# Attention and a gated MLP in one kernel: visits of the late units in one piece, and row sums of the first units over a 65th column

## The chip, the cores and the metric

One core of one Trainium2 chip runs the whole kernel. The time is device time in microseconds (us) of one execution; a version's time is the median of its runs. The engines are named as the profile names them: PE (TensorE matmuls), PEld (its weight loads), DVE (VectorE), ACT (ScalarE), POOL (GpSimd), SP (SyncE, which issues DMAs).

## What is computed

```python
for c in range(nc):                       # 24 chunks of 32 queries, seq 768
    q_c = q[:, :, c_start:c_end]
    k_ctx = k[:, :, l_start:r_end]        # 16 keys before, the chunk, 8 behind
    k_full = np.concatenate([mem_k, k_ctx], axis=2)   # and 8 memory keys: 64
    scores = scale * np.matmul(q_c, k_full.transpose(0, 1, 3, 2))
    a = np.exp(scores - np.max(scores, axis=-1, keepdims=True))
    a = a / (np.sum(a, axis=-1, keepdims=True) + 1e-09)
    out[:, :, c_start:c_end] = np.matmul(a, v_full)
x = out.transpose(0, 2, 1, 3).reshape(B * S, H * D)   # 3072 x 512
rms = np.sqrt(np.mean(x * x, axis=-1, keepdims=True) + 1e-6)
xn = x / rms * rms_g
g, val = xn @ w_gate, xn @ w_val                      # 512 -> 1536
result = (g * sigmoid(g) * val) @ w_out               # 1536 -> 512
```

There are 4 batches of 8 heads with head size 64.

## The kernel before, in words

**Attention.** The work is cut into 32 units: a batch, half of its sequence and a pair of heads. A unit's scores (tile `s`) are 128 rows by 6 chunks of 64 keys. DVE takes the row maxima (`mx`), subtracts them (`pe`), ACT takes the exponential in place, DVE sums the rows (`r`), adds 1e-9, takes the reciprocal and multiplies; PE transposes (`pT`), ACT copies the transposed tiles into SBUF (`pt`), and PE multiplies with v (`o`). The first eight units (`NE` = 8) supply the tokens of blocks 0 and 1 and are done at the start; their sums are taken for two units at a time (128x12). The other 24, the late units, go as 12 pairs in "visits" in between the products of the MLP.

**MLP.** The 3072 tokens are eight blocks of 384. The products are done in a reduced format (fp32r) with each operand split into a high and a low part, so each product is three matmuls: `xh`, `xl` are the parts of x, `wh`, `wl` those of a weight, `hh`, `hl` those of the hidden activations. `pg` is the product with w_gate, `pv` the one with w_val (12 matmuls each for a block and a column tile), `po` the one with w_out (9). Blocks 2 and later split their x and their weights by other code (tiles `kh`, `ks`, `os`, `sh`), and the last four blocks go as two "supers" of two blocks each, whose products are combined to save some (`mga`, `mva`, `mge`, `mve` and so on).

**Order.** Each engine runs its instructions in program order. Up to the end of block 1's first products the order is one written list of tokens, `ORDER`: a letter is a step and its number the unit or tile. U loads q and k, V loads v, Z a weight; S, M, a, E, d, n, P, C/m, O are scores, maximum, subtraction, exponential, row sums with reciprocal, multiplication, transposes, copies, product with v. J (two ACT passes), F, f, I, H, L open, clamp, sign, shift, round and subtract a piece of weight; an `a` behind f puts the sign on ACT, otherwise it is DVE's.

The blocks 0, 2 and 3 then run by gaps: gap 2n lies after the n-th `pg`, 2n+1 after `pv`, 2n+1.5 after the `po` that follows it. `VISITS` says for each gap which steps of the late pairs come there: `p` (transposes of the older pair with ACT's copies), `s` (scores of the next pair with their maximum, subtraction and exponential), `o` (product with v of the older pair in two tiles `oe` and `oo`, ACT's copies of both into the MLP's input `xT`, the squares of the copies on ACT, their addition on DVE, and row sums and reciprocals for the newer pair), `n` (the norm). The second half's tile `oo` lies in the PSUM bank with the tag that `stage_o2` is given; `pg` and `pv` use the tags "g" and "v".

In the supers the order of visits is in a table of its own. There `late_r` has ACT square the copies and DVE add the squares at once.

Of the kernel before, what the change touches and what calls it, by code (L numbers as in the profile page):

```python
# [8 lines left out]
F32 = mybir.dt.float32  # L9
# [5 lines left out]
ALU = mybir.AluOpType  # L15
# [3 lines left out]
B, H, S, D = 4, 8, 768, 64  # L19
# [3 lines left out]
KC = NM + LC + CH + RC  # L23
DM, FF = 512, 1536
P = 128
# [4 lines left out]
NJ = NC // 2  # L30
# [4 lines left out]
NE = NG * 2  # L35
# [4 lines left out]
YMAX = 0x1DFE / 0x1000 * 2.0 ** -96  # L40


VISITS = {0: {1: 's', 5: 'ps', 5.5: 'o', 7: 'ps', 7.5: 'o', 9: 'n', 10: 'n', 11: 'n'}, 2: {5: 'ps', 5.5: 'o', 17: 'ps', 17.5: 'o', 19: 'n', 20: 'nn'}, 3: {3: 'ps', 3.5: 'o', 7: 'ps', 7.5: 'o', 9: 'n', 9.5: 'n', 10: 'n', 11: 'ps', 11.5: 'o', 15: 'ps', 15.5: 'o', 17.5: 'n', 18: 'n', 19: 'n'}}
PAIRS = ((1, 2), (3, 4), (5, 6), (7, 8), (0, 9), (10, 11))
NR = 30

# [21 lines left out]


ORDER = """  # L70
U0 U1 U2 Z U3 S0 U4 M0 a0 Z S1 U5 E0 S2 M1 a1 Z V0 E1 M2 J d0 U7 S3 fa V1 F S4 n1 a2 V2 n0 E2 V3 M3 J I U6 P0 a3 H
M4 S5 E3 f m0a F C0a d1 Z J P1 V4 O0 M5 m1a a4 C1a S7 a5 E4 n2 E5 n3 Q0 P2 B0 I O1 C2a d2 Z m2a V5 B1 P3 V7 H V6 D0
C3a L O2 m3a n4 Q1 L P4 B2 A1g D1 p0 C4a M7 S6 Q2 n5 J A2g a7 O3 M6 m4a F q0 a6 Q3 P5 f E6 A3g O4 E7 D2 C5a d3 p2 Q4
G3 m5a B3 O5 I B4 y0 n6 Z H q1 D4 B5 p1 D3 J P6 n7 p3 D5 P7 C6a f Q5 q2 m6a L Y0 m7a F O6 C7a A5 z0 f O7 Q6 r0 B6 I
q3 Q7 B7 A6 p4 Z h0 p5 A7 D6 G7 D7 p6 y1 H j0 p7 F q5 k0a I J q4 L Z q6 l0 H q7 F J Y1 f o0 L z1 F r1 I h1 g2 J f Z
j1 I H k1a Z L v2 fa l1 F r2 H I h2 o1 J Z j2 L H F f g3 k2a L J v3 r3 l2 I h3 f Z H g4 J L F j3 o2 I f Z H v4 k3a F
J l3 r4 o3 I h4 F Z fa L g5 j4 k4a I v5 J l4 Z r5 o4 h5 f H H L g6 j5 J F v6 r6 L k5a l5 g7 I h6 J Z o5 r7 j6 H f g8
L k6a fa l6 F v7 F I h7 I o6 Z H J j7 Z L v8 r8 k7a H l7 g9 F h8 L J f o7 j8 I v9 k8a Z H l8 r9 F h9 g10 J j9 L f
v10 I o8 r10 Z H f J F g11 k9a F l9 h10 o9 j10 r11 I g12 L Z k10a fa l10 H I v11 Z h11 L Z H J L o10 Z J F j11 f v12
k11a r12 J l11 f F g13 I F H I J L o11 h12 H j12 J L v13 F r13 k12a f fa f I g14 l12 H I L Z H o12 Z F h13 j13 I L Z  # L80
v14 k13a H l13 J r14 o13 h14 f J L F fa I g15 j14 k14a H v15 r15 l14 L h15 J F o14 I j15 R0 fa F g16 H I k15a L H
l15 v16 r16 L h16 o15 j16
"""


# [1 line left out]
def tile_kernel(ctx: ExitStack, tc: tile.TileContext, q, k, v, w_gate, w_val, w_out, rms_g, out, out_t):  # L87
    nc = tc.nc
    const = ctx.enter_context(tc.tile_pool(name="const", bufs=1))
    p1 = ctx.enter_context(tc.tile_pool(name="p1", bufs=1))  # L90
    p2 = ctx.enter_context(tc.tile_pool(name="p2", bufs=2))
    p3 = ctx.enter_context(tc.tile_pool(name="p3", bufs=3))
# [12 lines left out]
    early = early_cm.__enter__()  # L105
# [34 lines left out]
    st = {}  # L140
    pts = [early.tile([P, NT, 4, 2, CH], F32, name=f"pt{i}") for i in range(2)]
    late, late_cm = {}, {}

    def late_buffers(i):

# [86 lines left out]
    def stage_mb(u):  # L232
        d = st[u]
        s3, mx = d["s3"], d["mx"]
        if u >= NE:
            pe = p1.tile([P, NJ, KC], F32, name=f"pe{u}", tag=f"pe{u % 2}")
        else:
            if ("pe", u // 2) not in st:
                st["pe", u // 2] = early.tile([P, 2, NJ, KC], F32, name=f"pe{u}", tag=f"pe{u // 2 % 2}")
            d["pair"] = st["pe", u // 2]  # L240
            pe = d["pair"][:, u % 2]
        nc.vector.tensor_tensor(out=pe, in0=s3, in1=mx.unsqueeze(2).broadcast_to([P, NJ, KC]), op=ALU.subtract)
        d["p"] = pe

# [8 lines left out]
    def stage_da(u):  # L253

        if u >= NE:
            pe = st[u]["p"].unsqueeze(1)
            rr = p2.tile([P, 1, NJ], F32, name=f"r{u}", tag="r")
            st[u]["r"] = rr[:, 0]
        else:
            pe = st[u]["pair"]  # L260
            rr = early.tile([P, 2, NJ], F32, name=f"r{u}", tag="r")
            for i in range(2):
                st[u - u % 2 + i]["r"] = rr[:, i]
        if units[u][1]:
            nc.vector.memset(pe[64:P, :, NJ - 1, LC + CH:LC + CH + RC], 0.0)
        else:
            nc.vector.memset(pe[0:64, :, 0, NM:NM + LC], 0.0)
        pe, r = pe.rearrange("p u j k -> p (u j) k"), rr.rearrange("p u j -> p (u j)")
        nc.vector.tensor_reduce(out=r, in_=pe, axis=AX.X, op=ALU.add)
        nc.vector.tensor_scalar(out=r, in0=r, scalar1=1e-9, scalar2=None, op0=ALU.add)  # L270
        nc.vector.reciprocal(out=r, in_=r)

    def stage_db(u):
        pe, r = st[u]["p"], st[u]["r"]
        nc.vector.tensor_tensor(out=pe, in0=pe, in1=r.unsqueeze(2).broadcast_to([P, NJ, KC]), op=ALU.mult)

    def stage_p(u, tag=None):
        d = st[u]
# [34 lines left out]
                        on_pe(nc.tensor.matmul(o2[cp][64 * hh:64 * hh + 64, o:o + CH], lhsT=st[u]["v"][r, j, hh],  # L313
                                               rhs=pt[r, j, hh ^ u % 2], start=True, stop=True))

    def late_r(pair, x):

        g = units[pair[0]][2]
        o2 = st["o2"]
        for u in pair:  # L320
            st.pop(u)
        xc = x[g // 2].rearrange("p g (j c q) -> p g j c q", c=2, q=CH)
        for cp in (1, 0):
            nc.scalar.copy(xc[:, :, :, cp], o2[cp][:, 0:HT].rearrange("p (g j q) -> p g j q", g=2, q=CH))  # L324
        for i in range(g, g + 2):
            s = obuf(f"sq{i}")[:, 0:HT]
            nc.scalar.activation(s, x[i // 2][:, i % 2], AF.Square)
            if i:
                nc.vector.tensor_tensor(out=s, in0=s, in1=late["ss"], op=ALU.add)
            late["ss"] = s  # L330

    def late_n(x, parts=1):

# [215 lines left out]
    make_identity(nc, ident)  # L549
    for t in pts:  # L550
        nc.vector.memset(t, 0.0)
    nc.gpsimd.tensor_scalar(out=rg, in0=rg, scalar1=DM ** 0.5, scalar2=None, op0=ALU.mult)
    nc.vector.memset(mhalf, -0.5)
    nc.vector.memset(onef, 1.0)
# [14 lines left out]
    def late_steps():  # L569


        pairs = [(u, u + 1) for u in range(NE, len(units), 2)]
        for n in range(len(pairs) + 1):
            old = pairs[n - 1] if n else ()
            cur = pairs[n] if n < len(pairs) else ()
            new = pairs[n + 1] if n + 1 < len(pairs) else ()
            own = bool(old) and old[0] >= 3 * 2 * NG
            if old and old[0] % NG == 0:
                if old[0] // NG in (5, 7):
                    late_x["x"] = [p1.tile([P, 2, HT], F32, name="x1", tag="wy"),  # L580
                                   late["tmp"][:, 0:2 * HT].rearrange("p (g t) -> p g t", g=2)]
                else:
                    t = p1.tile([P, NKT, HT], F32, name="xT", tag="x")
                    late_x["x"] = [t[:, 0:2], t[:, 2:4]]
                late_x[old[0] // NG] = late_x["x"]
            x = late_x.get("x")
            if old:
                with tc.high_priority():
                    for i, u in enumerate(old):
                        stage_p(u, None if i or own else "g")  # L590
                    for u in old:
                        stage_c(u)
                yield "p"
            if cur:
                with tc.high_priority():
                    stage_s2(cur)
                    for u in cur:
                        stage_m(u)
                    for u in cur:
                        stage_e(u)  # L600
            for u in new:
                load_qk(u)
            if old:
                if cur:
                    yield "s"
                with tc.high_priority():
                    stage_o2(old, None if own else "v")
                    late_r(old, x)
            norm = late_n(x, 1 if cur else 2) if n and n % 2 == 0 else ()
            behind = ExitStack()  # L610
            if norm:
                with tc.high_priority():
                    next(norm)
                behind.enter_context(tc.issue_after(last_of(nc.vector)))
            if own and norm and cur:
                for u in cur:
                    load_v(u)
                yield "o"
                next(norm)
                yield "n"  # L620
                with tc.high_priority():
                    for u in cur:
                        stage_d(u)
                yield "d"
            else:
                with tc.high_priority(), behind:
                    for u in cur:
                        stage_d(u)
                for u in cur if n else ():
                    load_v(u)  # L630
                yield "o" if old else "s"
            for _ in norm:
                yield "n"
# [670 lines left out]
```

## Time and profile before

| what | value |
|---|---|
| runs | 652.34, 652.45 and 655.0 us, median 652.45 us |
| profiled execution | 652.04 us, of which the profile's span is 650.2 us |
| busy share of the span | PE 98%, PEld 93%, DVE 75%, ACT 56%, POOL 2% |
| chain that ended last | PE 94%, DMA 2%, ACT 2%, DVE 1% |

The profile shows the profiled execution; 1.84 us of its time lie around the span. A matmul's record begins where its columns begin to stream, and consecutive records overlap, so what a matmul costs is read from one start to the next.

### The profile page before, as it was taken

The page shows a single profiled execution, that of the slowest core. Times are in us where ns is not written, and L with a number is a line of the kernel's source. Part 1 is how long each engine was busy: PE and PEld are TensorE (multiplying, and loading weights), DVE is VectorE, ACT ScalarE, POOL GpSimd, SP SyncE. Part 2 cuts the span into 40 slices and gives each one's busy share as a digit, 9 for nine tenths or more (in the row PEclk, how much of TensorE's full clock was granted, in tenths as well). Part 3 has the DMA queues.
Part 4 walks back from the last instruction along what each step waited for, and adds up shares of the span by engine and source line. Part 5 has one row for each costly group of instructions (what it writes and reads, how often), then busy time and mean ns, then how long its engine had stood idle before and what let it go on. Part 6 is the DMA issues. An engine that isn't in the chain of part 4 may idle for free.

```text
span 650.2 us, 15459 instructions
## 1 busy us (share of the span) xinstructions
PE 638.2 (98%) x6110; PEld 603.9 (93%) x6110; DVE 489.4 (75%) x999; ACT 366.2 (56%) x691; POOL 13.8 (2%) x19
## 2 busy tenths in 40 slices
PE   6999999999999999999999999999999999999997
PEld 4789999999899999999999999999999999999997
DVE  6999899768698888876888865567679854544864
ACT  4998877744545546465565454555566443333463
POOL 0200000000000000000000000000000000000000
PEclk7999999999999999999999999999999999999999
DMA  8737544269797887265459998887878988887711
GB/s 322 295 131 258 191 162 162 111 221 322 222 383 284 302 303 266 79 208 204 134 168 368 356 314 289 268 285 223 264 224 275 302 275 253 255 252 253 251 36 73
DMA packets 94006, 155.14 MB, mean 239 GB/s; under 512 B 8048, under 2 KB 47344, under 8 KB 93936
## 3 DMA queue, kind: packets, MB, share of 16 engines
q1 hardware_dynamic: 91920, 150.93, 69.2%
q10 hardware_dynamic: 2016, 3.25, 1.4%
q8 instruction: 48, 0.79, 0.5%
q14 instruction: 22, 0.18, 0.1%
HBM read 114.03 MB, written 40.11 MB: 237 GB/s over the span
## 4 chain that ended last, share of the span: by engine, by line
PE 94%; DMA 2%; ACT 2%; DVE 1%; issue 0%; SPq 0%
PE po L529 16%; PE pg L473 16%; PE pv L473 15%; PE mga L1001 8%; PE pa L1084 8%; PE mva L1001 8%; PE pe L1084 4%; PE mge L1001 4%; PE mve L1001 4%; PE oe L313 2%; PE s L219 2%; PE pc L1084 2%; PE mvc L1001 2%; PE mgc L1001 2%; PE pT L282 1%; DMA ws<-in_moe_w_val_dram 1%
## 5 line engine op out<-in xcount | busy, mean ns | idle before, releaser
L473 PE MATMUL pg<-xh,wh_g 128*128 128x384 f32 x192 | 65.9, 343 | 0.0
L473 PE MATMUL pv<-xh,wh_v 128*128 128x384 f32 x192 | 64.9, 338 | 0.5 <-ACT xT L324 0.5
L473 PE MATMUL pg<-xh,wl_g 128*128 128x384 f32 x192 | 64.6, 337 | 0.0
L473 PE MATMUL pg<-xl,wh_g 128*128 128x384 f32 x192 | 64.6, 336 | 0.0
L473 PE MATMUL pv<-xh,wl_v 128*128 128x384 f32 x192 | 64.3, 335 | 0.0
L473 PE MATMUL pv<-xl,wh_v 128*128 128x384 f32 x192 | 64.2, 334 | 0.0
L1001 PE MATMUL mga<-x,r 128*128 128x384 f32 x288 | 58.0, 335 | 0.0
L1001 PE MATMUL mva<-x,r 128*128 128x384 f32 x288 | 57.7, 334 | 0.0
L529 PE MATMUL po<-wh_o,hh 128*128 128x512 f32 x141 | 55.9, 396 | 0.0
L529 PE MATMUL po<-wl_o,hh 128*128 128x512 f32 x141 | 55.6, 394 | 0.0
L529 PE MATMUL po<-wh_o,hl 128*128 128x512 f32 x141 | 55.6, 394 | 0.0
L1052 ACT CAST hho<-h 128x384 fp32r<-128x384 f32 x72 | 37.0, 514 | 32.7 <-PE pa L1084 19.0
L1001 PEld LDWEIGHTS mva<-x,r 128*128 128x128 f32 x288 | 50.6, 188 | 0.0
L1001 PEld LDWEIGHTS mga<-x,r 128*128 128x128 f32 x288 | 50.5, 188 | 0.1
L1084 PE MATMUL pa<-hho,r 128*128 128x384 f32 x192 | 50.3, 335 | 0.0
L1053 DVE TENSOR_TENSOR hlo<-h,hho 128x384 fp32r<-128x384 f32 x72 | 39.3, 555 | 13.3 <-ACT hho L1052 12.4
L181 ACT CAST hh<-t 128x384 fp32r<-128x384 f32 x45 | 23.2, 516 | 44.1 <-PE po L529 20.3
L473 PEld LDWEIGHTS pg<-xh,wh_g 128*128 128x128 f32 x192 | 36.1, 188 | 1.8
L473 PEld LDWEIGHTS pv<-xh,wh_v 128*128 128x128 f32 x192 | 36.0, 188 | 1.7 <-ACT xT L324 0.9
L473 PEld LDWEIGHTS pg<-xl,wh_g 128*128 128x128 f32 x192 | 36.1, 188 | 1.4 <-DVE xl L676 0.2
L473 PEld LDWEIGHTS pv<-xl,wh_v 128*128 128x128 f32 x192 | 36.0, 188 | 0.3
L473 PEld LDWEIGHTS pg<-xh,wl_g 128*128 128x128 f32 x192 | 36.0, 188 | 0.0
(195 smaller groups left out, 1561.3 us busy)
## 6 DMA issues: line engine op xcount, KB each, us to landing
r<-kg SPq DMA_DIRECT2D x84, 256.0 KB, 3.8
r<-kv SPq DMA_DIRECT2D x84, 256.0 KB, 3.6
r<-ko SPq DMA_DIRECT2D x84, 256.0 KB, 3.2
kv<-in_v_dram SPq DMA_DIRECT2D x24, 384.0 KB, 4.4
kv<-in_k_dram SPq DMA_DIRECT2D x24, 312.0 KB, 4.4
q<-in_q_dram SPq DMA_DIRECT2D x20, 192.0 KB, 4.2
ws<-in_moe_w_gate_dram SPq DMA_DIRECT2D x6, 512.0 KB, 3.7
ws<-in_moe_w_val_dram SPq DMA_DIRECT2D x6, 512.0 KB, 4.6
```

The source lines that it names most:

```text
L181: return nc.scalar.copy(out, in_)
L219: on_pe(nc.tensor.matmul(d["s"][a:a + CH, o:o + KC], lhsT=d["q"][r, c * CH:c * CH + CH], rhs=d["k"][r, c // 2, 40 * cp:40 * cp + KC], star ...
L282: on_pe(nc.tensor.transpose(out=t[:, i * P:(i + 1) * P], in_=pe[:, i * P:(i + 1) * P], identity=ident))
L313: on_pe(nc.tensor.matmul(o2[cp][64 * hh:64 * hh + 64, o:o + CH], lhsT=st[u]["v"][r, j, hh], rhs=pt[r, j, hh ^ u % 2], start=True, stop=True))
L473: on_pe(nc.tensor.matmul(ps[:, 0:HT], lhsT=weight(a, n, f, kt), rhs=xs[c][:, kt], start=kt == first and i == 0, stop=kt == last and i == 2))
L529: on_pe(nc.tensor.matmul(po[i], lhsT=h[a][:, i * P:(i + 1) * P], rhs=weight(c, "o", f), start=f == first and n == 0, stop=f == end and n = ...
L1001: on_pe(nc.tensor.matmul(bank[w, b], lhsT=r[:, a, kt], rhs=x[:, c, kt], start=bool(first) and kt == 0 and i == 0, stop=kt == 1 and i == 2, ...
L1052: nc.scalar.copy(hh, x)
L1053: nc.vector.tensor_tensor(out=hl, in0=x, in1=hh.bitcast(F32), op=ALU.subtract)
L1084: on_pe(nc.tensor.matmul(bank[c][i], lhsT=w[u][:, x, i * P:(i + 1) * P], rhs=uhl[u][y], start=p == 0 and n == 0 and m in (1, 2, 5), stop=p ...
```

## The change

Four things are changed. In blocks 0, 2 and 3 the step `o` moves from behind the `po` of its gap to the end of the visit ahead of it, at eight places, and its second tile moves from the bank of tag "v" to that of tag "g". In the supers, the addition of the squares of every second pair is held until the next visit (`hold`). For the first eight units the tile `pe` gets a 65th column, set to 1e-9 once at the start, so that the row sum includes it, and the multiplication writes to another tile (`pn`) from which the transposes read. And `ORDER` is another sequence of the same 465 steps; of the changes in it only the first line is shown. In it the second weight load stands ahead of the loads of unit 4, units 0 and 1 change places, and two of the signs move from DVE to ACT (`f` 19 and `fa` 8 become 17 and 10).

```diff
-VISITS = {0: {1: 's', 5: 'ps', 5.5: 'o', 7: 'ps', 7.5: 'o', 9: 'n', 10: 'n', 11: 'n'}, 2: {5: 'ps', 5.5: 'o', 17: 'ps', 17.5: 'o', 19: 'n', 20: 'nn'}, 3: {3: 'ps', 3.5: 'o', 7: 'ps', 7.5: 'o', 9: 'n', 9.5: 'n', 10: 'n', 11: 'ps', 11.5: 'o', 15: 'ps', 15.5: 'o', 17.5: 'n', 18: 'n', 19: 'n'}}
+VISITS = {0: {1: 's', 5: 'pso', 7: 'pso', 9: 'n', 10: 'n', 11: 'n'}, 2: {5: 'pso', 17: 'pso', 19: 'n', 20: 'nn'}, 3: {3: 'pso', 7: 'pso', 9: 'n', 9.5: 'n', 10: 'n', 11: 'pso', 15: 'pso', 17.5: 'n', 18: 'n', 19: 'n'}}
...
-U0 U1 U2 Z U3 S0 U4 M0 a0 Z S1 U5 E0 S2 M1 a1 Z V0 E1 M2 J d0 U7 S3 fa V1 F S4 n1 a2 V2 n0 E2 V3 M3 J I U6 P0 a3 H
+U1 U0 U2 Z U3 S1 Z U4 M1 a1 S0 U5 E1 S2 M0 a0 Z V0 E0 M2 J d0 U6 S3 n0 J V1 a2 P0 M3 U7 E2 n1 S4 C0a a3 m0a f V2 E3
...
+    pn = [early.tile([P, NJ, KC], F32, name=f"pn{i}") for i in range(3)]
+    pairs_pe = [early.tile([P, 2, NJ, KC + 1], F32, name=f"pe{i}") for i in range(2)]
...
-            if ("pe", u // 2) not in st:
-                st["pe", u // 2] = early.tile([P, 2, NJ, KC], F32, name=f"pe{u}", tag=f"pe{u // 2 % 2}")
-            d["pair"] = st["pe", u // 2]
-            pe = d["pair"][:, u % 2]
+            d["pair"] = pairs_pe[u // 2 % 2]
+            pe = d["pair"][:, u % 2, :, 0:KC]
...
-        nc.vector.tensor_scalar(out=r, in0=r, scalar1=1e-9, scalar2=None, op0=ALU.add)
+        if u >= NE:
+            nc.vector.tensor_scalar(out=r, in0=r, scalar1=1e-9, scalar2=None, op0=ALU.add)
         nc.vector.reciprocal(out=r, in_=r)
...
-        nc.vector.tensor_tensor(out=pe, in0=pe, in1=r.unsqueeze(2).broadcast_to([P, NJ, KC]), op=ALU.mult)
+        if u < NE:
+            st[u]["p"] = pn[u % len(pn)]
+        nc.vector.tensor_tensor(out=st[u]["p"], in0=pe, in1=r.unsqueeze(2).broadcast_to([P, NJ, KC]), op=ALU.mult)
...
+    def late_add(s):
+        nc.vector.tensor_tensor(out=s, in0=s, in1=late["ss"], op=ALU.add)
+        late["ss"] = s
+
-    def late_r(pair, x):
+    def late_r(pair, x, hold=False):
...
-            if i:
-                nc.vector.tensor_tensor(out=s, in0=s, in1=late["ss"], op=ALU.add)
-            late["ss"] = s
+            if not i:
+                late["ss"] = s
+            elif hold:
+                late["held"] = s
+            else:
+                late_add(s)
...
+    for t in pairs_pe:
+        nc.vector.memset(t[:, :, :, KC:], 1e-9)
...
                 with tc.high_priority():
+                    if "held" in late:
+                        late_add(late.pop("held"))
                     for i, u in enumerate(old):
                         stage_p(u, None if i or own else "g")
...
-                    stage_o2(old, None if own else "v")
-                    late_r(old, x)
+                    stage_o2(old, None if own else "g")
+                    late_r(old, x, own and n % 2 == 1)
```

How instructions now stand is shown at three places. First PE in the first of the eight visits, in block 0. `pT` are the transposes, `s` the scores, `oe`/`oo` the product with v, `po` the product with w_out. Only the first and last rows of each group are shown. Before:

```order
L282 MATMUL pT_1965<-ident,pe_1851 128x128 x3
L219 MATMUL s_1971<-kv_1648,q_1646 32x64 x2
...
L529 MATMUL po_788<-wh_o_1122,hh 128x512
...
L529 MATMUL po_790<-wh_o_1122,hl 128x512
L313 MATMUL oe_2044<-pt_1647,kv_1648 64x32 x2
...
L313 MATMUL oo_2045<-kv_1648,kv_1708 64x32 x2
L473 MATMUL pg<-xh_144,wh_g_1124 128x384
```

And of the change:

```order
L285 MATMUL pT_1964<-ident,pe_1850 128x128 x3
L221 MATMUL s_1970<-kv_1646,q_1644 32x64 x2
...
L316 MATMUL oe_2034<-pt_1645,kv_1646 64x32 x2
...
L316 MATMUL oo_2035<-kv_1646,kv_1707 64x32 x2
L539 MATMUL po_776<-wh_o_1133,hh 128x512
...
L539 MATMUL po_778<-wh_o_1133,hl 128x512
L483 MATMUL pg<-xh_151,wh_g_1135 128x384
```

The 24 small `oe` and `oo` rows have changed places with the nine `po`.

Next DVE near its start, at the row sums of the first pair of units and what follows them; `mx` are the maxima of later units, `wy` a piece of weight. Before:

```order
L230 TENSOR_REDUCE mx_266<-s_233 128x6
L267 MEMSET pe_199 64x2x16
L269 TENSOR_REDUCE r_271<-pe_199 128x12
L270 TENSOR_SCALAR r_271<-r_271 128x12
L271 RECIPROCAL r_271<-r_271 128x12
L422 TENSOR_SCALAR wy_268<-wy_268 128x512
L275 TENSOR_TENSOR pe_199<-pe_199,r_271 128x384
L242 TENSOR_TENSOR pe_335<-s_233,mx_266 128x384
L275 TENSOR_TENSOR pe_199<-pe_199,r_271 128x384
```

And of the change:

```order
L232 TENSOR_REDUCE mx_272<-s_239 128x6
L267 MEMSET pe_128 64x2x16
L269 TENSOR_REDUCE r_277<-pe_128 128x12
L272 RECIPROCAL r_277<-r_277 128x12
L278 TENSOR_TENSOR pn_125<-pe_128,r_277 128x384
L242 TENSOR_TENSOR pe_129<-s_239,mx_272 128x6x64
L232 TENSOR_REDUCE mx_321<-s_285 128x6
L278 TENSOR_TENSOR pn_126<-pe_128,r_277 128x384
```

The row L270 is gone, the clamp of a weight piece (L422) stands further back, and the products are written to `pn`.

Last DVE in the first super, at the first addition of squares there; `e` and `spare` are sums of PE's products. Before:

```order
L977 TENSOR_TENSOR e_5198<-mge,e_5198 128x384
L977 TENSOR_TENSOR spare<-mge,spare 128x384
L329 TENSOR_TENSOR sq_5298<-sq_5298,sq_5296 128x384
L977 TENSOR_TENSOR e_5219<-mve,e_5219 128x384
L984 TENSOR_TENSOR h_5125<-spare,e_5219 128x384
```

And of the change:

```order
L991 TENSOR_TENSOR e_5197<-mge,e_5197 128x384
L991 TENSOR_TENSOR spare<-mge,spare 128x384
L991 TENSOR_TENSOR e_5218<-mve,e_5218 128x384
L320 TENSOR_TENSOR sq_5297<-sq_5297,sq_5295 128x384
L998 TENSOR_TENSOR h_5124<-spare,e_5218 128x384
```

The sum `e` of `mve` now stands ahead of the addition of squares.

## Rows read from the trace of the kernel before

**Rows 1.** The page: busy time by engine; shares of the chain that ended last.

```profile
PE 638.2 (98%) x6110; PEld 603.9 (93%) x6110; DVE 489.4 (75%) x999; ACT 366.2 (56%) x691; POOL 13.8 (2%) x19
...
PE 94%; DMA 2%; ACT 2%; DVE 1%; issue 0%; SPq 0%
```

**Rows 2.** Windows, early stretch: length, busy PE, PEld, DVE, ACT, POOL; PEclk, DMA share, GB/s.

```profile
8.40:14.40 6.00, 4.32 (x144) 3.78 (x144) 5.01 (x12) 3.91 (x6) 0.00 (x0) 0.52 1.04 407
...
18.00:24.05 6.05, 5.05 (x127) 4.15 (x126) 5.89 (x14) 5.92 (x14) 0.00 (x0) 0.93 1.04 414
24.05:43.27 19.22, 19.12 (x252) 16.84 (x253) 18.62 (x40) 18.55 (x38) 5.66 (x5) 1.00 0.39 144
```

**Rows 3.** Waits of PE over the span: total, times, longest.

```profile
PE s L203 <- DMA k<-in_k_dram: 4.1, 5, 1.2
...
PE mve L1001 <- DVE e L977: 0.7, 1, 0.7
...
PE pv L473 <- ACT xT L324: 0.5, 1, 0.5
```

**Rows 4.** Timeline of DVE, 8 to 25 us: start, duration.

```profile
10.47 0.95 DVE L269 TENSOR_REDUCE r<-pe 128x12 f32<-128x768 f32 x1
11.45 0.17 DVE L270 TENSOR_SCALAR r<-r 128x12 f32<-128x12 f32 x1
11.66 0.23 DVE L271 RECIPROCAL r<-r 128x12 f32<-128x12 f32 x1
```

**Rows 5.** The chain that ended last, 8 to 46 us: start, duration.

```profile
6.73 7.22 DMA ws<-in_moe_w_val_dram
13.97 0.69 ACT ws L417
...
25.12 0.97 PE s L203 x48
```

**Rows 6.** The chain that ended last, 155 to 176 us: start, duration.

```profile
155.53 2.08 PE pv L473 x12
...
159.37 2.26 PE po L529 x9
...
163.17 2.32 PE pg L473 x12
165.49 0.47 ACT xT L324
...
166.01 2.35 PE pv L473 x12
```

**Rows 7.** Timeline of ACT, 208 to 217 us.

```profile
213.24 0.53 ACT L247 ACTIVATE pe<-pe 128x384 f32<-128x384 f32 x1 [0.76 <-DVE pe L242]
213.79 0.51 ACT L181 CAST hh<-t 128x384 fp32r<-128x384 f32 x1
214.21 0.52 ACT L247 ACTIVATE pe<-pe 128x384 f32<-128x384 f32 x1
...
215.92 0.49 ACT L324 COPY xT<-oo 128x384 f32<-128x384 f32 x1
```

**Rows 8.** Timeline of PE, 215.2 to 215.8 us.

```profile
215.44 0.45 PE L473 MATMUL pg<-xh,wh_g 128*128 128x384 f32 x1
```

**Rows 9.** Timeline of DVE, 319 to 328 us.

```profile
320.29 2.20 DVE L361 SCALAR_TENSOR_TENSOR xT<-xT,rg,rr 128x384 f32<-128x384 f32 x4
322.41 0.69 DVE L866 TENSOR_TENSOR os<-wh_o,wl_o 128x512 f32<-128x512 f32 x1
323.01 1.02 DVE L230 TENSOR_REDUCE mx<-s 128x6 f32<-128x384 f32 x2
```

**Rows 10.** Timeline of PE, 321.2 to 325.4 us.

```profile
321.40 0.50 PE L529 MATMUL po<-wh_o,hh 128*128 128x512 f32 x1
```

**Rows 11.** Timeline of DVE, 398 to 403 us.

```profile
400.64 0.56 DVE L329 TENSOR_TENSOR sq<-sq,sq 128x384 f32<-128x384 f32 x1 [2.83 <-ACT sq L327]
401.12 0.55 DVE L977 TENSOR_TENSOR e<-mve,e 128x384 f32<-128x384 f32 x1
```

More of the change, by code (lines that the diff above doesn't have):

```diff
@@ L70 @@
 ORDER = """
-U0 U1 U2 Z U3 S0 U4 M0 a0 Z S1 U5 E0 S2 M1 a1 Z V0 E1 M2 J d0 U7 S3 fa V1 F S4 n1 a2 V2 n0 E2 V3 M3 J I U6 P0 a3 H
[L72 to L80, printed above, removed]
@@ L81 @@
-v14 k13a H l13 J r14 o13 h14 f J L F fa I g15 j14 k14a H v15 r15 l14 L h15 J F o14 I j15 R0 fa F g16 H I k15a L H
-l15 v16 r16 L h16 o15 j16
+U1 U0 U2 Z U3 S1 Z U4 M1 a1 S0 U5 E1 S2 M0 a0 Z V0 E0 M2 J d0 U6 S3 n0 J V1 a2 P0 M3 U7 E2 n1 S4 C0a a3 m0a f V2 E3
+F fa P1 d1 S5 C1a M4 m1a I J O0 n2 Z a4 V3 P2 H M5 V5 S6 E4 F V4 n3 B0 a5 m2a L E5 C2a I O1 Q0 d2 H P3 V7 B1 V6 S7
+C3a D0 Z Q1 n4 O2 m3a D1 A1g J M6 P4 L Q2 O3 M7 m4a a6 A2g C4a p1 a7 Q3 n5 q1 E7 A3 P5 E6 B3 G3 d3 m5a O4 C5a B2 O5
+n6 B4 y0 F Q4 P6 D2 B5 q0 D4 m6a p2 D5 C6a p0 D3 Q5 Y0 n7 J F P7 A5 p3 z0 f C7a O6 I m7a O7 r0 Z B6 Q6 q3 Q7 A6 h0
@@ new lines @@
+q2 A7 p5 f G7 D6 p4 B7 j0 p6 H y1 D7 q5 k0a F q4 I q7 L Z H p7 f Y1 l0 q6 L z1 o0 J I r1 Z H F f h1 g2 J j1 L I fa F
+Z v2 r2 k1a J l1 I g3 H Z fa L F H I o1 h2 L Z J j2 r3 v3 k2a H l2 J f F o2 I L Z h3 f J g4 F j3 I k3a v4 H r4 Z H
+l3 L g5 f J L o3 h4 F fa j4 r5 F v5 I k4a Z l4 g6 I h5 H j5 Z J o4 r6 L f v6 k5a J l5 F I g7 h6 H Z j6 o5 r7 L v7
+k6a H l6 h7 L J o6 j7 f g8 fa F I v8 r8 Z H F I k7a J g9 l7 Z L h8 o7 H j8 F f v9 k8a r9 J l8 L o8 h9 F J j9 I g10 f
+Z k9a H v10 l9 fa r10 I L g11 Z F J I o9 h10 H r11 Z j10 L g12 k10a fa l10 F h11 I v11 H Z Z H L J o10 j11 J L F Z
@@ L83 @@
+r12 J v12 f f k11a f l11 g13 I h12 j12 H F J F v13 L I I H fa o11 L r13 F I g14 Z k12a J Z l12 h13 o12 H j13 fa F H
+I v14 k13a r14 Z l13 L h14 o13 L J j14 J f F g15 H f k14a l14 L v15 F J I r15 H F o14 I fa L R0 h15 I H g16 j15 H L
+k15a l15 v16 r16 L h16 o15 j16
 """
```

## The prediction

> **What bounds the kernel now.** The page first: PE is busy for 98% of the span and makes up 94% of the chain that ended last; DVE is at 75%, ACT at 56% [rows 1]. So PE's own work sets the time, and a change can gain only where PE stands idle, or where its matmuls run at a worse pace than the same matmuls elsewhere. The windows show where it stands. From 24.05 us on it is dense (19.12 of 19.22 us busy, and as dense behind). Ahead of that it is not: 4.32 of 6 us at a granted clock of 0.52 (the lower of TensorE's two levels, 1.2 GHz) in the stretch from 8.4 us, and 5.05 of 6.05 at 0.93 in the stretch up to 24.05, where DVE (5.89) and ACT (5.92) are both full [rows 2]. The waits of PE then name what is left: 4.1 us for the first loads of k, 0.7 us in a super for a sum `e` of DVE, 0.5 us for a copy `xT` of ACT [rows 3]. The last two are the only waits of note behind 24 us, and both stand beside steps that this change moves.
>
> The chain of the early stretch tells what sets the 24 us: the landing of the first piece of w_val (issued at 6.73 us, 7.22 us long), ACT's opening of it at 13.97, then ACT and DVE by turns until PE's dense work, in which the eighth unit's scores are 0.97 us at 25.12 [rows 5]. Loads run at full share of the DMA engines there (1.04, 407 GB/s) [rows 2].
>
> **The visits.** PE does transposes, scores, `po`, `oe`/`oo`, `pg`. Its own work stays the same. What differs is how often it goes from the small matmuls to large ones. Twelve `pv` in plain sequence take 2.08 us; the twelve `pg` behind `oe`/`oo`, which have the same size, take 2.32 [rows 6]. The break costs 0.24 us. `po` behind the scores (2.26 us for nine) pays a break of its own. After the change the small ones stand together, and only `po` behind them pays. I take the whole 0.24 eight times: -1.9 us. What bounds it: nothing, if `oe`/`oo` behind the scores pay for themselves (a change of operands between small ones is shown by no row), and 0.24 if they don't; I take the upper end since the small matmuls already change their operands at each row within the visit.
>
> The one wait on `xT` comes in this place too: `pg` ends at 165.49, ACT's copy `xT` ends at 165.96, and `pv` then takes 2.35 [rows 6], since it writes the bank of tag "v" from which that copy reads. With the second tile in the bank of "g" and a whole `po` behind it, `pv` need not wait for it: -0.5 of waiting, and a part of the 0.27 by which this `pv` is longer than the plain one. I take -0.6.
>
> The new wait is `pg`'s, since it now writes the bank that the copy of `oo` reads. In the visit at 210 us ACT does its exponentials at 213.24 and 214.21 with a cast `hh` between, and the copy of `oo` ends at 216.41 [rows 7]; `pg` starts at 215.44 [rows 8] and doesn't care, as it isn't its bank. In the changed order the cast is behind the copies. The exponentials start as before (they wait for DVE's subtraction of scores that are no earlier), 0.5 us each, so the second ends near 214.3, and two copies by 0.4 us start to start end near 215.05. `pT`, scores, `oe`/`oo` and `po` sum to the same, so `pg` would start at 215.4: it has about 0.36 us to spare. The Trainium skill, "PSUM — Partial Sum Buffer", section "PSUM bank collisions raise a hardware error", says that different engines may not touch one bank and group of partitions at once and that a semaphore has to guard it by bank, which is why even a copy that reads other columns would hold `pg`; by it alone the wait exists in all eight visits, and what it costs is the row's matter.
>
> One visit has nothing to spare. At 320 us DVE is held until 323.01 by four steps of the norm (2.20 us) and a sum for a weight (0.69) [rows 9]; the scores end by 321.4, when `po` starts [rows 10]. The maxima could start there and start 1.5 us later; the subtractions, exponentials and copies behind them are late by as much, and less the 0.36 to spare `pg` waits about 1.1 us. Behind `pg` on PE stands everything else, so this counts in full.
>
> **The held addition.** In the first super DVE has the addition of squares at 400.64, after 2.83 us of waiting for ACT's squares, and the sum `e` at 401.12 is queued behind it [rows 11]; PE's `mve` waits 0.7 us for `e` [rows 3]. The change puts `e` ahead of the addition, which itself waits for nothing at the next visit. So -0.7 us. Nobody needs the sum of squares before the norm of the second pair. The other supers have the same move without a wait to remove: 0.
>
> **The first units.** Removed are four additions of 1e-9 on DVE. One takes 0.17 us and holds its queue from 11.45 to 11.66, so 0.21 us [rows 4]; three lie ahead of the dense stretch: -0.63 us of DVE's queue. Two signs move from DVE to ACT, one addition from POOL to DVE; they lie behind 24 us, where PE is dense, and I cost them at nothing as long as the halves of the weights come before PE asks for them (if not, each is about half a microsecond). Two memsets of 128x12 at the start lie in DVE's wait for the first scores: nothing. The sums over 65 columns of 12 rows read 12 elements more out of 768; at 0.95 us for the 768 [rows 4] that is 0.015 us each: nothing.
>
> The order itself: the load of w_val goes ahead of unit 4's, by 512 KB at 407 GB/s 1.3 us earlier. But both openings now stand on ACT ahead of the second pair's exponentials and wait for that landing, near 12.7 us; by walking ACT's and DVE's queues with the rows' durations, the third exponential ends near 15.9 us, DVE idles about a microsecond there, and the multiplication before the fifth transpose comes at 23.9 us where it was 23.4. Against that the eighth unit's scores (0.97 us [rows 5]) have moved ahead of it into time in which PE stands idle, and one triple of `pg`/`pv` more (0.52 us) is done before the first `po`. I come to -0.45 us, and as bounds -2 (w_val's 1.3 us and the 0.63 both come through) and +1 (the microsecond on DVE is lost in full and the gains aren't).
>
> **Sum.** -1.9 -0.6 +1.1 -0.7 -0.45 = -2.55 us. From the profiled execution's 652.04 us (its span 650.2 and 1.84 around it) that is 649.5; the median of the runs shown is 652.45, 0.41 above it, and gives 649.9. I say 649.7. A measurement of this kernel can tell about 0.5% (3.3 us) from no change, so the forecast lies inside that.
>
> **Rivals.**
> *The early stretch gains the most of it.* The chain begins at w_val's landing [rows 5]; if that piece of chain just moves by 1.3 us and DVE loses its 0.63, dense work begins 1.5 us earlier than worked out above: 648.2 us. For it speaks that both DVE and ACT are full from 18 us on [rows 2], so each row taken off counts; against it, that the opening now stands in front of an exponential.
> *The visits give nothing.* The break is paid by `oe`/`oo` behind the scores, whose transposed operands come from ACT's copy only just before. Then 1.9 is lost: 651.6 us, and up to 652.5 if the early stretch loses its microsecond as well.
> *Rows of 65.* DVE's subtraction, sum and multiplication for the first units work on rows that begin at every other alignment. If these rows are slower, four steps of about 0.5 us and one of 0.95 for each pair lengthen; a pace lower by one eighth on 2.9 us costs 0.36 for a pair, 1.1 us for the three ahead of the dense stretch, against 0.63 saved: 650.8 us. No row here has such rows, and the bound below is nothing. The Trainium skill, "Vector Engine (DVE) Microarchitecture Reference", section "5.2 Measured stream behaviour on trn2 (trn3 not measured)", says that a port has its full pace only for pairs of neighbouring words that begin on an even word, and gives 1.30 ns a column for pairs on odd ones against 1.054. An estimate by that page, for half of the rows, is an eighth. No run here shows it yet.
> *Slower: `pg` waits for the bank at every visit.* If something is queued on DVE or ACT ahead of the copies in each, as in the visit at 320 us, `pg` waits 1.1 us at the other seven too: +7.7, 657.4 us. It decides (over 655.7) from 0.9 us a visit on. Against it stand the 0.36 us to spare by [rows 7, 8].
>
> **How the numbers follow.** The forecast (649.0 to 650.6) gets 0.47, the early gain 0.21, the visits without gain 0.16, rows of 65 0.10, the bank 0.06. Faster by over 0.5% (below 649.2): a fifth of the forecast (0.09) and nearly all of the early gain (0.20), 0.29. Slower by over 0.5%: the bank, and 0.01 for other things, 0.07. The rest is 0.64. The range reaches from a little below the early gain (647.6, with its bound of -2) to the end of the second rival (652.3).
>
> **What would show it.** `pg` behind a visit takes 2.1 us, `po` 2.26; no wait of `pv` on `xT` near 165; a wait of `pg` on ACT's `xT` of about 1 us near 325 and none above 0.2 elsewhere; no wait of `mve` on `e`; the first dense transposes near 24.4 us and the first `po` near 43.3. A `pg` that waits in most visits, or a start of the dense stretch off by over a microsecond, makes the prediction wrong.

## The result and the profile after

The changed kernel takes 657.22 us (median of 20 runs, 654.55 to 662.52), the kernel before 653.30 (20 runs, 652.26 to 655.07). The ratio of the two is 1.0058, 95% interval 1.0042 to 1.0074: slower, outside the predicted range, and on the side that had 0.07. The runs of the change also spread more than twice as far.

The profiled execution took 658.87 us, 1.65 above the median; its span is 656.8 us, 6.6 more than before's. Where they come from is read from one landmark of PE's timeline to the next; both executions are put side by side here (start in us of the first `po`, of the transposes of each of the eight visits, and of those of the first super):

```
             before   after   later by
first po      43.27   44.23     0.96
visit 1      157.46  158.33     0.87
visit 2      168.20  168.26     0.06
visit 3      209.80  210.53     0.73
visit 4      251.07  251.88     0.81
visit 5      286.82  290.08     3.26
visit 6      303.02  308.82     5.80
visit 7      319.56  325.16     5.60
visit 8      335.80  342.80     7.00
first super  376.34  383.84     7.50
end          650.20  656.80     6.60
```

Three visits lose nearly all of it: the fourth (at 251 us) 2.45, the fifth (290) 2.54, the seventh (325) 1.40. The second loses 0.67, against 0.81 that the first gains. The waits of PE name three releasers for them (total, times, longest):

```profile
PE s L205 <- DVE r L269: 1.7, 1, 1.7
PE oe L316 <- ACT kv L183: 1.4, 1, 1.4
PE pg L483 <- ACT x L331: 1.4, 1, 1.4
PE pT L285 <- issue: 1.2, 1, 1.2
PE oe L316 <- issue: 1.0, 1, 1.0
...
PE oo L316 <- issue: 0.6, 1, 0.6
```

Before, `pv`'s wait for `xT` and `mve`'s for `e` stood in this list [rows 3]; both are gone, as forecast. New are a wait of `oe` for ACT's copy `kv`, the forecast wait of `pg` for the copy of the second tile, and four waits for "issue": time in which PE waited for nothing that the profile shows. The early stretch, by windows (length, busy PE, PEld, DVE, ACT and POOL, granted clock, DMA share, GB/s):

```profile
8.40:14.40 6.00, 3.69 (x99) 2.91 (x94) 5.32 (x11) 2.72 (x5) 0.00 (x0) 1.00 1.04 400
...
18.00:24.05 6.05, 4.96 (x164) 3.94 (x157) 5.92 (x14) 5.90 (x13) 0.00 (x0) 1.00 1.01 381
24.05:43.27 19.22, 17.78 (x244) 16.38 (x233) 18.09 (x38) 17.48 (x36) 3.85 (x4) 1.00 0.35 124
```

The stretch behind 24.05 us, where PE was dense before (19.12 of 19.22 us, [rows 2]), now has 1.4 us of idle PE in it; 1.2 of them are one wait for "issue" within the three transposes of a unit.

The visit at 290 us on PE's timeline (start, duration, in brackets the idle time before):

```profile
292.37 0.23 PE L316 MATMUL oo<-kv,kv 64*64 64x32 f32 x2
293.57 0.25 PE L316 MATMUL oe<-pt,kv 64*64 64x32 f32 x2 [0.98 <-issue]
...
295.06 0.63 PE L539 MATMUL po<-wl_o,hh 128*128 128x512 f32 x1
295.49 0.63 PE L539 MATMUL po<-wh_o,hl 128*128 128x512 f32 x1
...
298.39 0.34 PE L483 MATMUL pg<-xh,wh_g 128*128 128x384 f32 x1
```

The product with v stops for about a microsecond in the midst of its small matmuls with both operands there. Behind it the nine `po` come 0.43 us apart, where they are 0.23 apart elsewhere: 3.75 us instead of 2.2. The windows of the `po` behind the visits at 251 and 290 us show why (PEclk is the granted clock):

```profile
core 0: us, PE busy (x) PEld busy (x) DVE busy (x) ACT busy (x) POOL busy (x), PEclk, DMA share, GB/s
256.76:260.34 3.58, 3.58 (x15) 2.79 (x10) 1.12 (x2) 2.69 (x7) 0.00 (x0) 0.58 1.00 316
294.64:298.39 3.75, 3.75 (x15) 2.94 (x10) 2.58 (x10) 1.90 (x5) 0.00 (x0) 0.54 1.00 325
```

The clock that was granted is near the lower of its two levels (1.2 GHz), after PE had stood idle for 1.4 and 1.0 us amid small matmuls. The visit at 251 us has its idle time from ACT, whose copy `kv` is queued behind a cast `kh` that waits for DVE:

```profile
252.84 0.47 ACT L183 COPY pt<-pT 128x384 f32<-128x384 f32 x1
254.39 0.40 ACT L860 CAST kh<-ks 128x256 fp32r<-128x256 f32 x1 [1.08 <-DVE ks L855]
254.71 0.47 ACT L183 COPY kv<-pT 128x384 f32<-128x384 f32 x1
```

```profile
255.23 0.25 PE L316 MATMUL oe<-pt,kv 64*64 64x32 f32 x2 [1.43 <-ACT kv L183]
```

At 325 us `pg` starts when ACT's copy of `oo` has ended (ACT, then PE), as the prediction worked out for this visit:

```profile
330.48 0.99 ACT L247 ACTIVATE pe<-pe 128x384 f32<-128x384 f32 x2 [2.63 <-DVE pe L242]
...
331.73 0.48 ACT L331 COPY x<-oo 128x384 f32<-128x384 f32 x1
```

```profile
332.26 0.44 PE L483 MATMUL pg<-xh,wh_g 128*128 128x384 f32 x1 [1.38 <-ACT x L331]
```

### The profile page after: what moved, and what is told of

The parts are those of the page before. It is cut to its first block, busy times and chain, and to the rows that moved or that the text cites. A ratio compares the mean times of both kernels' runs of the same rounds, so it can differ in the third digit from the quotient of the medians.

```text
span 656.8 us, 15458 instructions
## 1 busy us (share of the span) xinstructions
PE 640.4 (98%) x6110; PEld 607.9 (93%) x6110; DVE 488.1 (74%) x996; ACT 368.7 (56%) x693; POOL 12.3 (2%) x18
## 4 chain that ended last, share of the span: by engine, by line
PE 85%; DVE 7%; DMA 4%; ACT 2%; issue 1%; SPq 1%; DVEq 0%; ACTq 0%
PE pg L483 13%; PE po L539 13%; PE pv L483 12%; PE mga L1015 8%; PE pa L1098 8%; PE mva L1015 8%; PE mge L1015 4%; PE mve L1015 4%; PE pe L1098 4%; PE pc L1098 2%; PE mvc L1015 2%; PE mgc L1015 2%; PE oe L316 2%; PE s L221 2%; DMA kv<-qp 2%
## 5 line engine op out<-in xcount | busy, mean ns | idle before, releaser
L539 PE MATMUL po<-wh_o,hl 128*128 128x512 f32 x141 | 57.1, 405 | 0.0
```

What stands on the lines that cost most here:

```text
L539: on_pe(nc.tensor.matmul(po[i], lhsT=h[a][:, i * P:(i + 1) * P], rhs=weight(c, "o", f), start=f == first and n == 0, stop=f == end and n = ...
```

## Experiments

Two theories were put against each other at first, A: the visits lose the time by waits on other engines and on the bank; B: the early stretch does. A third, C, was that PE's waits for "issue" are the cause. All times are medians; the kernel before ran beside each (653.3 to 653.8 us).

**The visits alone** (`visits_only`), the early part and the held addition as before (all eight visits; only the first two are shown, here and in the next edit):

```diff
-... 5: 'ps', 5.5: 'o', 7: 'ps', 7.5: 'o' ...
+... 5: 'pso', 7: 'pso' ...
...
-stage_o2(old, None if own else "v")
+stage_o2(old, None if own else "g")
```

> The kernel before with only the visits changed (the eight products with v behind the scores, second tile in the bank of tag g). Theory A, the visits lose the time: o waits for ACT's kv copy behind a cast kh in the visits at 251 and 290 us, PE's clock falls to its lower level after such a wait, and pg waits 1.4 us for xT in the visit at 325 us; then 4 to 6 us slower than before. Theory B, the early stretch (new order and 65 columns) loses it: then 2 us faster than before. Theory C, idle times of PE that the profile calls issue come wherever small matmuls crowd: slower by 1 to 3 us, with such idle times in several visits.

657.77 us, ratio 1.0067 (1.0051 to 1.0083). **The early part alone** (`early_only`), which is the rest of the change without the held addition:

```diff
-... 5: 'pso', 7: 'pso' ...
+... 5: 'ps', 5.5: 'o', 7: 'ps', 7.5: 'o' ...
...
-stage_o2(old, None if own else "g")
+stage_o2(old, None if own else "v")
-late_r(old, x, own and n % 2 == 1)
+late_r(old, x)
```

> The change without its visits and without the held addition: the new order of the first blocks and the 65th column alone. Theory A: about 0.9 us slower than before, as the first po of the changed kernel came 0.96 us later. Theory B: 4 us slower. Theory C: up to 1.5 us slower, through the idle times of 1.2 and 0.3 us near 20 and 27 us.

652.96 us, ratio 0.9993 (0.9979 to 1.0006). B falls: the visits cost 4.2 us, and the early part alone differs from before by no more than its interval.

**Three visits put back** (`split3`):

```diff
-... 17: 'pso' ... 3: {3: 'pso' ... 11: 'pso' ...
+... 17: 'ps', 17.5: 'o' ... 3: {3: 'ps', 3.5: 'o' ... 11: 'ps', 11.5: 'o' ...
...
+stage_o2(old, None if own else "v" if n in (4, 5, 7) else "g")
```

> The changed kernel with three of its eight visits (at 251, 290 and 325 us) put back as they were before. Theory A: these three lost 2.45, 2.54 and 1.4 us of the profiled run, so 5 to 6 us faster than the changed kernel, 0 to 2 us faster than before. Theory B: as the changed kernel, 4 us slower than before. Theory C: half of the loss stays, 2 us slower than before.

652.87 us, ratio 0.9998 (0.9986 to 1.0011), 4.35 faster than the change: the loss is in these three, by the median. Its profile still has a wait of `oo` for "issue" in the second visit (0.9 us).

**The casts moved away** (`keep_later`):

```diff
-... 14: 1792, 22: 1024 ... 2: 1536, 5: 2048 ...
+... 18: 1792, 22: 1024 ... 5: 3584 ...
```

> The changed kernel with two portions of the sums of weights (tiles ks and kh) moved from ahead of the visits at 251 and 290 us to behind them, so that no cast kh stands between ACT's two copies pt and kv; all visits stay in one piece. Theory A: the wait of oe on kv and the fall of the clock at both visits are gone, 4 to 5 us faster than the changed kernel, about as before. Theory B: no difference from the changed kernel. Theory C: the wait of 1.4 us and one fall of the clock are gone, the idle time of 1 us at 290 us and the fall of the clock behind it stay, so 2.5 us faster than the changed kernel.

657.78 us, ratio 1.0064 (1.0045 to 1.0084): no gain. In its profile the fourth and fifth visits are clean, but `po` now waits 0.78 and 1.52 us for `hl` and `hh` at 247 and 279 us, and the sixth visit stops for "issue" for 1.49 us with the slow `po` behind it. The move made waits of its own, so it doesn't tell A from C.

**What "issue" is.** Each place at which PE stopped so was counted in PE's stream: weight loads, matmuls (the trace has 6110 of each) and PE's semaphore instructions. Position in the stream, less 192 (the place of the first step), over 256, in the profiles of five kernels:

```
after        s at 20.74: 2.00    pT at 27.05: 3.01    oo at 171.56: 13.01   oe at 293.57: 22.00
visits_only  s at 13.70: 1.00    s at 21.49: 2.00     oo at 173.45: 13.00   oe at 293.12: 22.01
split3       pT at 27.13: 3.01   oo at 173.10: 13.01
keep_later   s at 20.45: 2.00    pT at 27.09: 3.01    oo at 171.54: 13.01   oo at 310.17: 24.01
early_only   pT at 26.55: 3.01
```

Each lies at a multiple of 256 instructions, and so do all 41 such stops in the 17 profiles of this study. The page of the changed kernel has a queue that carries that stream (queue, kind: packets, MB, share):

```profile
q8 instruction: 48, 0.79, 0.5%
```

0.79 MB in 48 packets are 16.4 KB each; the trace has 12,481 instructions of PE, 260 a packet. It also has the packets one by one, each of the same size, one for a step (us; `pad32` and `mended_front` are runs below):

```
                   PE stands from   packet             PE goes on   behind the packet's end
after, oo              171.00       169.09 to 170.14     171.56        1.42
after, oe              292.59       291.32 to 292.29     293.57        1.29
pad32, oo              219.75       220.38 to 221.34     222.70        1.35
mended_front, o         24.49        24.91 to  25.86      27.11        1.25
```

At all 41 stops PE goes on 1.1 to 1.6 us behind the end of the packet of that step. At 760 other steps it doesn't wait; there the packet had ended over 1.6 us earlier at 745 and 0.9 to 1.6 us earlier at the rest. So what PE waits for is its next instructions.

A visit's transposes, scores and product with v are some 400 instructions. In one piece PE takes 256 of them in 1.6 to 2.0 us; with `po` in between, in about 4. In the second visit the packet for its second step starts as PE passes the first, at 169.09, and PE can go on 2.5 us later. Two of the steps lie within the second and the fifth visit, one within each other but the third, which has its first step five instructions behind its start; there the packet for the other had ended 3.2 us ahead, and PE doesn't stop. Two experiments move the steps, by small matmuls that nobody reads, ahead of block 0's first `pg`.

**13 matmuls, 52 instructions** (`pad13`), after which each visit has one step in it:

```diff
+            if blk == 0 and n == 0:
+                pad = psum_m("g", "pad")
+                for _ in range(13):
+                    on_pe(nc.tensor.matmul(pad[0:64, 0:64], lhsT=ident[:, 0:64], rhs=ident[:, 0:64], start=True, stop=True))
             g = moe_in("g", f, xs)
```

> The changed kernel with 13 small matmuls that nobody reads put ahead of block 0's first pg near 150 us (52 instructions of PE's stream, some 0.5 us of PE). Idle times of PE called issue were seen at every 256 instructions of its stream, where two such places lie within one visit: in the visits at 168 and 290 us. With 52 instructions more each visit has one such place. Theory C, PE waits there for its next instructions: the idle time of 0.6 to 1 us at 168 and that at 290 us are gone, with the fall of the clock behind the latter; 1.5 to 3 us faster than the changed kernel. Theory A, only waits on ACT and DVE and the bank: no idle time changes its place, 0.5 us slower than the changed kernel.

655.73 us, ratio 1.0039 (1.0021 to 1.0058). The matmuls cost more than was expected: from the tenth group of `po` to the last ahead of the visits it is 51.33 us where the change has 49.36, so 2.0 us. Against that the visits gave back 3.5 (657.22 - 655.73 + 2.0). The profiles agree: the second and the fifth visit, from the transposes to the `pv` behind them, take 7.66 us each where the change has 8.52 and 10.40. In its profile no "issue" stands behind 27 us, and the two other waits stay (PE):

```profile
PE pT L285 <- issue: 1.5, 1, 1.5
PE pg L483 <- ACT x L331: 1.4, 1, 1.4
PE oe L316 <- ACT kv L183: 1.1, 1, 1.1
```

**32 matmuls, 128 instructions** (`pad32`; the same edit with 32):

> As the run with 13, with 32 small matmuls (128 instructions, half a step of 256). Theory C: two places at a multiple of 256 now lie in the visits at 158, 251, 306, 323 and 341 us and the idle times are there and no longer at 168 and 290 us, where the second place is at the visit's end; 1 to 5 us slower than the changed kernel, more where the clock falls behind them. Theory A: 1 us slower, by the matmuls themselves, idle times where they were.

674.52 us, ratio 1.0303 (1.0280 to 1.0326): 17.3 us slower than the change, 4.2 of it the matmuls' own (53.56 against 49.36 as above). PE's waits:

```profile
PE oo L316 <- issue: 7.7, 4, 2.9
...
PE oe L316 <- issue: 2.9, 2, 1.5
...
PE po L539 <- issue: 0.9, 1, 0.9
```

Seven visits stop, each at a step of 256 (12.00, 17.00, 20.01, 23.00, 25.01, 27.00, 29.01 by the count above), 11.5 us in all. One of them, and a `po` behind it, at a granted clock of 0.50 over its nine (223.05 to 227.06 us):

```profile
222.70 0.43 PE L316 MATMUL oo<-kv,kv 64*64 64x32 f32 x4 [2.94 <-issue]
...
224.50 0.63 PE L539 MATMUL po<-wh_o,hh 128*128 128x512 f32 x1
```

**The same 32 in the kernel before** (`before_pad32`):

> The kernel before, visits untouched, with the 32 small matmuls near 150 us that cost the changed kernel 17 us (by the first products behind them about 4.2 us are the matmuls' own). Theory C: where po stands between scores and oe/oo, PE takes 256 instructions of a visit in about 4 us and not in 1.8, so its next instructions are there in time and only the matmuls' own time is added: 657 to 659 us, no idle time called issue in the visits. If the place of the steps of 256 costs the same in any visit: 668 to 672 us.

658.56 us, ratio 1.0075 (1.0059 to 1.0090): 4.9 us slower, of which 4.2 are the matmuls. Steps lie within all visits there too, but with `po` in between one visit alone stops:

```profile
PE oo L313 <- issue: 0.9, 1, 0.9
```

C holds, and it is the one piece that makes these steps cost something.

**The bank** (`v7`), the tag of one visit:

```diff
-stage_o2(old, None if own else "g")
+stage_o2(old, None if own else "v" if n == 7 else "g")
```

> The changed kernel with the second tile of the one visit at 325 us in the bank of tag v instead of g. If pg's wait of 1.4 us there comes from the bank that the copy of oo reads, it is gone: 1.2 to 1.5 us faster than the changed kernel. If the copies hold pg for another reason, no difference.

655.61 us, ratio 1.0036 (1.0015 to 1.0058), 1.6 faster than the change. The two intervals overlap, but the rows agree: `pg` doesn't wait there in the profile, and that visit takes 7.68 us where the change has 9.29. **The wait for kv** (`split4`), the fourth visit alone in two parts, by the edit of `split3` for 17:

> The changed kernel with the visit at 251 us alone in two parts as before. There oe waits 1.4 us for ACT's kv copy behind a cast kh, and in two of four profiles the clock fell behind the wait for 1.5 us more. If that visit is worth what its rows show: 1.5 to 3 us faster than the changed kernel (654.2 to 655.7 us). If the delay only moves to another place: no difference.

655.25 us, ratio 1.0034 (1.0022 to 1.0046), 2.0 faster; in the profile that visit takes 7.86 us for 10.73, of which 1.4 were the slow `po`. The others stay in its list:

```profile
PE pg L483 <- ACT x L331: 1.4, 1, 1.4
PE oe L316 <- issue: 1.2, 1, 1.2
PE oo L316 <- issue: 0.9, 1, 0.9
```

**All mended, with added matmuls.** `mended` has the fourth visit in two parts, the tag v for the fourth and seventh, and the 13 matmuls; the next two differ in where and how these are made, the last has before's order of the first blocks:

```diff
+stage_o2(old, None if own else "v" if n in (4, 7) else "g")
...
mended_front:  ORDER begins with "W13 U1" (13 matmuls at the start, none near 150 us)
mended_cheap:  pad[0:1, 0:1], lhsT=ident[:, 0:1], rhs=ident[:, 0:1]
mended_old:    ORDER of the kernel before
```

> The changed kernel with what the theories name taken away: 13 small matmuls as above, the visit at 251 us in two parts as before (its o waits 1.4 us for kv), and the tag v for the visits at 251 and 325 us. Theory A and C together: 4 to 6 us faster than the changed kernel, 1 to 2 us faster than before; the remaining six visits in one piece each save 0.2 us. If something else is behind the loss, it stays above before.

> The mended kernel with its 13 small matmuls at the very start, where PE waits for the first k, and not near 150 us, where they cost 2 us. The steps of 256 lie in the visits as in the mended kernel; those of the first 50 us move by 52 instructions. Theory C: 2 us faster than the mended kernel, 651 to 651.5 us, if the early steps don't come to lie worse; if they do, up to 1.5 us of it is lost between 20 and 30 us.

> The mended kernel with its 13 small matmuls near 150 us made on one column and one row of weights. If their cost of 2 us is in the 64 columns of weights and data, 1 to 1.5 us faster than the mended kernel (652 us); if it is a fixed cost for each, no difference. The visits are clean of idle times called issue either way.

> The mended kernel with the first blocks' order of the kernel before, the 65th column kept. If the new order is worth the 0.5 us that the change without its visits gained, 0 to 0.5 us slower than the mended kernel (653.3 to 654 us). If PE's early idle times called issue (1.2 to 1.7 us at the fifth transposes in seven runs with the new order) come from the new order alone, 1 us faster (652 us).

653.34 (ratio 0.9997, 0.9982 to 1.0013), 652.98 (0.9990, 0.9972 to 1.0009), 653.32 (0.9994, 0.9982 to 1.0006) and 654.14 us (1.0009, 0.9999 to 1.0019). All are as before's; none gains the 1 to 2 us that were hoped for. In all four the one-piece visits are free of these waits and take 0.2 us less each, but for 0.4 us within the eighth's `po` in three of them, at a step of 256 (29.0 by the count). `mended` still pays 2 us for its matmuls. `mended_front` doesn't, but its early part came 2.5 us later (first `po` at 46.59 against 44.11), as its expectation's other branch has it:

```profile
27.11 1.55 PE L302 MATMUL o<-pt,vw 128*64 128x64 f32 x24 [2.62 <-DVE wl_v L454]
```

The profile puts this wait down to `wl_v`, which `o` does not read. It lies at 3.01 by the count, and PE goes on 1.25 us behind the packet's end, so it is a step of 256 as well. Two more waits of this profile (1.23 us at 13.33 and 0.87 at 20.90) lie at 1.01 and 2.01. `mended_cheap` pays 1.1 for them, and in it and in `mended_old` the held addition has not moved: DVE has it ahead of `e` as before, and PE waits for `e` (DVE, then PE, of `mended_cheap`):

```profile
403.69 0.56 DVE L320 TENSOR_TENSOR sq<-sq,sq 128x384 f32<-128x384 f32 x1 [2.83 <-ACT sq L334]
404.16 0.55 DVE L991 TENSOR_TENSOR e<-mve,e 128x384 f32<-128x384 f32 x1
```

```profile
404.77 0.44 PE L1015 MATMUL mve<-x,r 128*128 128x384 f32 x1 [0.69 <-DVE e L991]
```

**The held addition pinned** (`hold_pinned`), in the kernel before:

```diff
+                if "held" in late:
+                    with tc.issue_after(last_of(nc.vector)):
+                        late_add(late.pop("held"))
                 with tc.high_priority():
```

> The kernel before with the addition of squares held and pinned behind the sum e on DVE, nothing else. If mve's wait of 0.7 us for e is only that addition ahead of it: no such wait, 0.7 to 0.9 us faster than before (652.7 us). If e itself is late: no difference.

652.35 us, ratio 0.9987 (0.9975 to 0.9999), 0.9 us faster, barely clear of its interval, and no wait of `mve`. Held without the pin, `e` stands ahead of the addition in the change and in `mended`, and behind it in `keep_later`, `mended_cheap` and `mended_old`, each with `mve`'s wait of 0.7 us. So the gain is the order of these two, and holding alone doesn't decide it.

**Four visits in one piece** (`select2`): the first, third, sixth and seventh (tag v), the others in two parts, the addition pinned, nothing added:

```diff
-... 7: 'pso' ... 17: 'pso' ... 3: {3: 'pso' ... 15: 'pso' ...
+... 7: 'ps', 7.5: 'o' ... 17: 'ps', 17.5: 'o' ... 3: {3: 'ps', 3.5: 'o' ... 15: 'ps', 15.5: 'o' ...
...
+stage_o2(old, None if own else "v" if n in (2, 4, 5, 7, 8) else "g")
```

> The changed kernel with four of the eight visits in one piece (158, 210, 306 and 325 us, the last with the tag v) and four in two parts (168 and 290, where two steps of 256 instructions lie within a visit, 251, which waits for kv, and 341), no small matmuls added, and the held addition pinned behind the sum e on DVE. If the places named are the whole of the loss: what the early part gives alone (653.0 us), less 0.2 for each of the four visits, 0.5 for pv's wait and 0.8 for mve's: 650.5 to 651.5 us, faster than before and than the change. If single pieces lose time elsewhere: 653 us or more.

651.63 us, ratio 0.9978 (0.9967 to 0.9989): faster than before by 1.7 us and than the change by 5.6, and 0.1 above the range that was expected. Its page has PE at the least busy time of the three, and its list has none of the waits in visits:

```profile
PE 637.5 (98%) x6110; PEld 605.0 (93%) x6110; DVE 489.7 (75%) x996; ACT 368.7 (57%) x693; POOL 12.1 (2%) x18
```

```profile
PE pT L285 <- issue: 1.8, 1, 1.8
...
PE po L539 <- DVE hl L516: 0.6, 1, 0.6
...
PE pv L483 <- DVE t L507: 0.4, 1, 0.4
```

## Why the prediction was wrong

**The step that failed** is the sentence on the visits that PE's "own work stays the same" and that what differs is only how often it goes from small matmuls to large. It took PE's supply of instructions for free. A visit in one piece asks for 256 instructions in 1.7 us, and where two steps of 256 lie in it, the next are not there in time: 0.6 and 1.0 us in the second and fifth visit of the profile, and 1.5 more where the clock falls behind it. By `pad13` the two come to 3.5 us at the median; in `pad32`, with stops in seven visits, the loss grows by another 13 us. No rival had it, and neither of the signs that the prediction named for being wrong (a `pg` that waits in most visits, a dense stretch off by over a microsecond) points at it. The one that ended slower named the bank at every visit; the bank waits in one.

**A wait dismissed.** For `kv` the prediction had no term, since before `o` came 2.3 us later and never waited. In one piece it waits wherever ACT's copy is late: 1.4 us in the profile, and 1.4 more in the slow `po` behind it; 2.0 in all by `split4`.

**Terms that held.** The break between small and large: clean visits take 0.2 us less (7.66 for 7.86; `po` 2.18 for 2.26, `pg` 2.11 for 2.22), forecast 0.24. `pv`'s wait of 0.5 us near 165 is gone. `pg`'s wait at 325 us was put at 1.1 and is 1.38 (1.6 by `v7`), and no other visit waits for the bank. The early part was put at -0.45 us; alone it gives 653.54 - 652.96 = 0.6 with no difference by its interval. Its path was another than walked, though, and that its size came out is luck: DVE was not what held the fifth transposes, which stopped at a step of 256 in eleven of the twelve profiles with the new order, for 0.4 to 1.8 us; in the twelfth, `mended_front`, the `o` behind them stopped there. Rows of 65 cost nothing: in the changed kernel the subtraction and the multiplication have the same mean as before (552 and 551 ns), and the sum 966 ns for its 780 columns, 12 more than before's 954 for 768. Groups of DVE, 4 to 24 us (busy us, mean ns, idle before):

```profile
L242 DVE TENSOR_TENSOR pe<-s,mx 128x384 f32<-128x384 f32 x6 | 3.3, 552 | 0.1
L269 DVE TENSOR_REDUCE r<-pe 128x12 f32<-128x780 f32 x3 | 2.9, 966 | 0.1
L278 DVE TENSOR_TENSOR pn<-pe,r 128x384 f32<-128x384 f32 x4 | 2.2, 551 | 0.0
```

The Trainium skill's figure for pairs that begin on an odd word ("Vector Engine (DVE) Microarchitecture Reference", section "5.2 Measured stream behaviour on trn2 (trn3 not measured)"), from which the prediction estimated an eighth, does not show in these runs of 64 words.

**A term right by its size, wrong by its reason.** `mve`'s 0.7 us: `hold_pinned` gives 0.9, but the holding itself does not settle that `e` stands ahead.

**Ledger.** Forecast were -2.55 us; 3.9 came, 6.5 off. Two steps of 256 with what follows them (3.5), `kv` (2.0) and 0.5 more at the bank make 6.0. Each of the three is a difference of medians whose intervals overlap or touch the change's, so each may be off by a microsecond; that they add up nearly is no proof of its own. The rest is within that, with one part known: the stretch from the eighth visit to the first super takes 41.04 us for 40.54, with that visit in one piece. In `select2`, which has it in two parts, it takes 41.47, so the form of the visit is not the whole cause. In the change the rows lose it at the last `po`, whose operand `hlast` comes late (its last rows lie 0.7 us further back); in `select2` `pv` waits 0.4 us for DVE's `t`, and that `po` loses 0.2. Why these come late stays open. So does what decides whether the clock falls: behind a wait of 1.4 us at 251 it fell in the change, behind one of 1.1 in `pad13` it did not; behind one of 1.0 at 290 it fell in the change, behind one of 1.2 there in `split4` it did not. Different numbers of these falls, 1.5 us each, would fit the spread of the change's runs; that was not shown.

## What to carry to other kernels

Small matmuls in one piece need their instructions as fast as they run: before putting blocks of them together, count the instructions between the large ones, and see whether PE stops at a 256th, also where the profile names an engine whose tile the waiting matmul doesn't read. Work that stands between two stages is also cover for the copies that the second needs; when it moves, go through every operand of the second, not only the one that is known to be tight. And where a scheduler orders two instructions, look at the order and don't infer it from the edit.

## What the runs showed of the hardware

PE's instructions come in steps of 256, and a step is not always there in time: PE stood there 41 times, 0.2 to 2.9 us each, in 15 of the 17 profiles of this study, and three times more in `mended_front` under another name. It went on 1.1 to 1.6 us behind the end of the 16.4 KB packet of that step. In the first 27 us (DMA share 1.0) all twelve profiles with the new order stop at the third step, for up to 2.6 us. The Trainium skill, "Runtime: NRT & Kernel Launch", section "Instruction fetch mechanics", has blocks of 256 instructions of which the next is fetched while one is executed; the places agree. It calls the crossing mostly hidden, which the large matmuls here show and the small ones don't. 13 matmuls of 64 columns on fp32 data cost 2.0 us in sequence, 0.15 each (1.1 us with one column, `mended_cheap`), far from the 0.01 to 0.02 us at which the scores of a visit follow each other.
